# Storing dw1 through GpSimd's queue in pieces of 7, 117 and 4 rows

## The chip, the core and the metric

The kernel runs on one core of one Trainium2 chip. The core has five engines with a queue of instructions each: TensorE (PE in the profile, its weight loads PEld), VectorE (DVE), ScalarE (ACT), GpSimd (POOL) and SyncE (SP). Data move between the device memory and the on-chip memory (128 partitions) by 16 DMA engines, which all queues share; a transfer issued from SP and one issued from GpSimd stand in different DMA queues (q1 and q0 in the profile) of the same 16 engines. The metric is the device time of one execution in microseconds (us).

## The reference

The kernel computes one decoding step of a gated mix of two branches and all its gradients, for one token x of 640 numbers and the upstream gradient `grad_out`:

```python
g = _sigmoid((x * gate_w).sum(-1, keepdims=True))
a = _A_ref(x, A_k_cache, A_v_cache, A_wq, A_wo)   # attention, 32 heads x 4096 cached keys x 128
b = _B_ref(x, B_w1, B_b1, B_w2)                   # 640 -> 1728 -> 640, act = h * tanh(softplus(h))
return g * a + (1 - g) * b
...
_out, _vjp = jax.vjp(_f, A_x, A_k_cache, A_v_cache, A_wq, A_wo, B_w1, B_b1, B_w2, gate_w)
_grads = _vjp(grad_out)
```

Outputs are the result, and the gradients of x, both caches, wq, wo, w1, b1, w2 and the gate. Everything is bf16. The caches are 32 MB each, and so are their gradients dK and dV, so that the kernel reads 82 MB and writes 82 MB. The gradient of w1, dw1, is a matrix of 640 x 1728 in bf16, 2.2 MB: the outer product of x and the gradient dh of the hidden layer. The gradients of x and of the gate are rows of 640 numbers, like the result.

## The kernel before, in words

**Tiles.** A head's cache is one tile of 128 partitions x 8192 bytes, 1 MB in all; partition p holds 32 consecutive keys. dK and dV leave in tiles of the same shape. Weights are held with 128 of the 640 rows (or a group of rows) over the partitions: `w1_sb` is [128, 5, 1728], so that partition r holds the five rows r, 128 + r, ..., 512 + r of w1, each a run of 3456 bytes, and on the device these five runs lie 128 rows apart. The gradient dw1 is written into the same tile (`m_dw1`, line 499, on VectorE, one instruction for each of the five rows), and stored through the view `dw1_v` of the same shape.

**Loops.** The main loop (line 743) goes over the heads h = 0 to 30, the last head follows it by hand (lines 855 to 896). In each pass TensorE transposes the next head's tiles, multiplies for scores and for their gradient; ScalarE evicts and computes the exponentials; VectorE builds dV (`dv_out`) and dK (`dk_out`), two instructions of line 598 each, into a buffer of the pool `outs` (four buffers, tile name `o_sb`); from head 28 or 29 on the loads' own buffers (`Kn`, `Vn`) are used, since no more loads come. Heads go in groups of four; once a group, its parts of dwq and dwo are made and stored. The second branch's work stands in a list `mq`, from which `mlp_some` takes a few pieces in each pass; the five `m_dw1` are the last of it.

**Order and queues.** The order of instructions on each engine is that of the Python code; a framework adds the semaphore waits. All large transfers, loads and stores, are issued by SP in program order, and each waits for its data, for its buffer, and for the transfer eight places ahead of it. GpSimd issues a few small ones: the load of b1 in two parts, five small moves for the hidden layer, the last 64 rows of dw2 (line 800), db1 (line 802), and at the end three rows of results. DMAs issued from GpSimd use eight semaphores in turn as well.

**Around the change.** The last `m_dw1` runs in pass 26. In pass 30 (`h == H - 2`), after `dv_out(h, 1)` has issued its store on SP, SP issues dw1 in two transfers, of three and of two of the five rows of each partition (lines 805 and 806). At the very end, VectorE gathers the results of 15 x 128 numbers (`fin`), TensorE transposes them, ScalarE evicts them to `fin_rows`, a tile of 15 partitions, and GpSimd stores five partitions each to the result, to the gradient of x and to that of the gate (lines 920 to 922).

Of the kernel before, what the change touches and what calls it, by code (L numbers as in the profile page):

```python
# [16 lines left out]
def kernel(  # L17
# [24 lines left out]
    nc = tc.nc  # L42
    P = 128
    _, H, Sk, Dh = A_k_cache.shape
    D = A_x.shape[-1]
    F = B_w1.shape[1]
    assert Dh == P and Sk == 32 * P and D % P == 0 and H % 4 == 0 and H >= 16
    J = Sk // P
    RC = D // P
# [25 lines left out]
    dw1_v = out_6.rearrange("(rc r) f -> r rc f", r=P)  # L75
# [9 lines left out]
    out0_rows = out_0.rearrange("a b (c p) -> (a b c) p", p=P)  # L85
    out1_rows = out_1.rearrange("a b (c p) -> (a b c) p", p=P)
# [60 lines left out]
    w1_sb = const.tile([P, RC, F], BF16, name="w1_sb")  # L147
# [59 lines left out]
    def g_q(g):  # L207
        gp = groups[g]
        ps = grp([P, GD], F32, "q_ps")
        for rc in range(RC):  # L210
            nc.tensor.matmul(ps[:], lhsT=x_col_bf[:, rc:rc + 1].to_broadcast([P, P]),
                             rhs=wqs[g][:, rc, :], start=(rc == 0), stop=(rc == RC - 1))
        nc.scalar.copy(gp["q_row"][:], ps[:])
# [32 lines left out]
    def g_qpair_cp(g):  # L246
        pair_cp(qz, groups[g].pop("pair"), 4)

    def g_docol(g):
        groups[g]["col"] = col_mm(groups[g]["do_row"])  # L250

    def g_dopair(g):
        groups[g]["pair"] = pair_mm(groups[g].pop("col"))

    def g_dopair_cp(g):
        pair_cp(doz, groups[g].pop("pair"), 5)
# [25 lines left out]
    def f_new(g):  # L282
        gp = groups[g]
        gp["o_bf"] = grp_sb.tile([P, G], BF16, name="o_bf", tag="o_bf")
        gp["dq_bc"] = grp_sb.tile([P, GD], BF16, name="dq_bc", tag="dq_bc", bufs=1)

    def f_diag(g, a=0, b=G):
        gp = groups[g]
        if b == G:
            gp["o_sel"] = grp_sb.tile([P, G, P // 4], F32, name="o_sel", tag="o_sel", bufs=1)  # L290
            nc.vector.tensor_tensor(gp["o_sel"][:], seg[:].unsqueeze(1).to_broadcast([P, G, P // 4]),
                                    gp["dqo"][:, 1, :].unsqueeze(2).to_broadcast([P, G, P // 4]), ALU.mult)
        gp["dq_diag"] = g_diag(gp["dqo"][:, 0, :], scale, a, b)
# [76 lines left out]
    def f_dwq(g, c, a=0, b=G):  # L370
        cs = slice(a * Dh, b * Dh)
        nc.vector.tensor_scalar(wqs[g][:, c, cs], groups[g]["dq_bc"][:, cs], x_col_f[:, c:c + 1], None, ALU.mult)  # L372

    def f_dwq_st(g):
        for k, (a, z) in enumerate(WQP):
            if g == z - 1:
                nc.sync.dma_start(dwq_v[:, :, a * GD:z * GD], wqp[k][:])
# [140 lines left out]
    def ev():  # L518
        trq.pop(0)()
# [6 lines left out]
    def k_pe(h, c):  # L526
        if h < H:
            tr_pe(h, kts, KT, c)

    def v_pe(h, c):  # L530
        if h < H:
            tr_pe(h, vts, VT, c)
# [8 lines left out]
    def k_rows(h):  # L541
        rows_mm(KT.pop(h), qz[:, h % G], True)
# [22 lines left out]
    def softmax(h):  # L565
        mx = s_ps.tile([P, P + 2], F32, name="mx", tag="mx")
        nc.tensor.transpose(mx[:, 0:P], dgms.pop(h)[:].to_broadcast([P, P]), ident_f[:])  # L567
        negM = small.tile([P, 1], F32, name="negM", tag="negM")
        nc.vector.tensor_reduce(negM[:], mx[:, 0:P], axis=AX.X, op=ALU.max, negate=True)  # L569
        return mx, negM  # L570

    def exps(h, negM):
        es[h] = small.tile([P, J], BF16, name="e_bf", tag="e_bf")
        zds[h] = small.tile([P, 2], F32, name="zd", tag="zd")
        nc.scalar.activation(es[h][:], sd[h][0], ACT.Exp, bias=negM[:], scale=scale, accum_out=zds[h][:, 0:1])  # L575

    def pjs(h):
        pj = small.tile([P, J], F32, name="pj", tag="pj", bufs=2)
        nc.vector.scalar_tensor_tensor(pj[:], in0=sd[h][1], scalar=1.0, in1=es[h][:],  # L579
                                       op0=ALU.mult, op1=ALU.mult, accum_out=zds[h][:, 1:2])  # L580

    def zd_mm(h, mx):
        nc.tensor.matmul(mx[:, P:P + 2], lhsT=ones_f[:], rhs=zds[h][:], start=True, stop=True)  # L583
# [37 lines left out]
    def dk_out(h, k):  # L621
        if h >= 0:
            out_half("k", h, dKv, ds4s[h], groups[h // G]["qs_row"], k)
# [12 lines left out]
    def dqo_red(h, x):  # L636
        if h >= 0:
            v = x[:].rearrange("p t r -> p (t r)")[:, 3:3 + 4 * (P - 1)].rearrange("p (s q) -> p s q", q=P - 1)
            nc.vector.tensor_reduce(groups[h // G]["dqo"][:, :, h % G],  # L639
                                    v[:, :, 0:P - 1:32].rearrange("p s (i c) -> p i s c", i=2),  # L640
                                    axis=AX.XY, op=ALU.add)
# [101 lines left out]
    for h in range(H - 1):  # L743
        g, hh = h // G, h % G
        nx, pv = g + 1 < NG, g > 0
        k_pe(h + 1, 2)
        ev()
        mx, negM = softmax(h)
        if hh == 3 and nx:
            g_qpair_cp(g + 1)  # L750
            g_docol(g + 1)
        dqo_red(h - 1, xs[h])
        k_pe(h + 1, 3)
        ev()
        exps(h, negM)
        dk_out(h - 1, 1)
        v_pe(h + 1, 0)
        if hh == 2 and nx:
            g_q(g + 1)
        v_pe(h + 1, 1)  # L760
        if hh == 3 and nx:
            g_dopair(g + 1)
            g_dopair_cp(g + 1)
        k_rows(h + 1)
        ev()
        ev()
        pjs(h)
        v_pe(h + 1, 2)
        ev()
        zd_mm(h, mx)  # L770
        if hh == 0 and pv:
            f_new(g - 1)
            f_diag(g - 1)
        elif h >= 2:
            mlp_some(0.9, False)
        v_pe(h + 1, 3)
        ev()
        probs(h, mx)
        if hh == 0 and pv:
            f_o4(g - 1)  # L780
            f_o4c(g - 1)
            f_bc(g - 1)
        dv_out(h, 0)
        k_pe(h + 2, 0)
        dq_o(h)
        v_rows(h + 1)
        rw_cp(h + 1)
        if h + 2 < H:
            ev()
        dv_out(h, 1)  # L790
        load_k(h + KBUFS)
        load_v(h + VBUFS)
        k_pe(h + 2, 1)
        if h + 2 < H:
            ev()
        if h == H - 4:
            assert dw2_next[0] == FCN
            for a, b in W2P:
                nc.sync.dma_start(dw2_v[:, a:b, :], w2_sb[:, a:b, :])
            nc.gpsimd.dma_start(out_8[FM:F, :], w2_sb[0:FT, FR, :])  # L800
            assert not any(k == "bc" for k, _ in mq)
            nc.gpsimd.dma_start(db1_row, dh_bc[0:1, :])
        if h == H - 2:
            assert not mq
            nc.sync.dma_start(dw1_v[:, 0:3, :], w1_sb[:, 0:3, :])
            nc.sync.dma_start(dw1_v[:, 3:RC, :], w1_sb[:, 3:RC, :])
        dk_out(h, 0)
        x_tr(h + 1)
        maxes(h + 1)
        if hh == 0:  # L810
            if nx:
                g_new(g + 1)
            if pv:
                l_pe(g - 1, 0, G)
                l_add(g - 1, g - 1, True)
                for t in range(G):
                    f_dwo(g - 1, t)
                f_dwo_st(g - 1)
                for c in range(2):
                    f_dx(g - 1, c)  # L820
                    f_dwq(g - 1, c)
        if hh == 1:
            if pv:
                for c in range(2, RC):
                    f_dx(g - 1, c)
                    f_dwq(g - 1, c)
                f_dwq_st(g - 1)
            if nx:
                w_pe("o", g + 1, 0)
                ev()  # L830
                w_pe("o", g + 1, 1)
                ev()
        if hh == 2:
            if g + 2 < NG:
                load_wo(g + 2)
            if not nx:
                for k in range(NWT):
                    w_pe("q", g, k)
                    ev()
            else:  # L840
                w_pe("o", g + 1, 2)
                ev()
                g_do(g + 1)
                g_qcol(g + 1)
                g_qpair(g + 1)
        if hh == 3:
            if g % 2 == 0 and g + 4 <= NG:
                load_wqp(g // 2 + 1)
            if nx:
                g_qs(g + 1)  # L850
        if h >= 2:
            mlp_some(0.9 if hh < 2 else 1.8)
            dw2_some(2)
# [63 lines left out]
    nc.tensor.transpose(fin_ps[:], fin_bf[:], ident_bf[:])  # L917
    fin_rows = const.tile([3 * RC, P], BF16, name="fin_rows")
    nc.scalar.copy(fin_rows[:], fin_ps[:])
    nc.gpsimd.dma_start(out0_rows, fin_rows[0:RC, :])  # L920
    nc.gpsimd.dma_start(out1_rows, fin_rows[RC:2 * RC, :])
    nc.gpsimd.dma_start(out9_rows, fin_rows[2 * RC:3 * RC, :])


# [28 lines left out]
```

## Time and profile before

| what | us |
|---|---|
| median of 3 runs (lowest, highest) | 404.74 (404.52, 404.89) |
| profiled execution, its own time | 404.96 |
| its span, first to last instruction | 403.2 |
| busy: PE, DVE, ACT, POOL | 305.9, 287.9, 232.4, 11.8 |
| DMA, mean over the span | 408 GB/s, 164.55 MB |
| last `m_dw1` on VectorE starts | 325.9 |
| dw1 issued by SP (two transfers) | 375.0, 375.5 |
| rows issued by GpSimd | 393.7, 394.2, 394.7 |

How to read it: times in the profile count from the span's start. A slice or column is one fortieth of the stretch shown. "L598 DVE o_sb" is line 598 of the kernel on VectorE, writing tile `o_sb`; "[4.39 <-DMA out_dram<-o_sb]" behind an instruction says that its engine stood idle 4.39 us before it, until that DMA landed. A transfer's issue (SPq, POOLq, DMA_DIRECT2D) and its landing are two things: the issue takes the queue well under 2 us, the landing can come many us later, since the transfer stands in the queue of the DMA engines. A transfer is dealt over DMA engines, and each of them adds to its semaphore when its part has landed; the landing is the last of the sixteen increments. The chain of waits is followed back from the last instruction; time after the last instruction of the chain, until the last semaphore is in, belongs to no engine.

### The profile page before, as it was taken

How to read it: one execution, taken by the hardware profiler on the slowest of the kernel's cores; microseconds unless marked ns; L12 is line 12 of the kernel's file. 1: busy time of each engine (PE TensorE's matmuls, PEld its weight loads, DVE VectorE, ACT ScalarE, POOL GpSimd, SP SyncE). 2: the span in 40 equal slices, each digit the busy share in tenths (PEclk: the TensorE clock that was granted, in tenths of full speed). 3: DMA queues.
4: the chain of work that ended last, by engine and by line, in shares of the span. 5: the costliest groups of instructions: out<-in, count | busy, mean ns of one | idle time of the engine just before them, and what ended most of it. 6: DMA issues, size and time to landing. Idle time of an engine off the chain costs nothing.

```text
span 403.2 us, 7688 instructions
## 1 busy us (share of the span) xinstructions
PE 305.9 (76%) x2930; PEld 207.0 (51%) x2945; DVE 287.9 (71%) x808; ACT 232.4 (58%) x468; POOL 11.8 (3%) x29
## 2 busy tenths in 40 slices
PE   2979989787897985876887779876886977677640
PEld 1556646464565663544555447544555645464420
DVE  2217738868678875769897956896997985679780
ACT  2466757754676563753668667765767655375220
POOL 3000001000000000000001200000000000000001
PEclk9999999988999998989998997988999899889555
DMA  7999999999999999999999999999999999999894
GB/s 274 428 416 423 417 424 415 417 423 424 422 422 426 423 414 424 424 418 428 422 423 428 424 418 424 427 418 423 422 419 424 425 417 425 426 422 377 360 389 153
DMA packets 28708, 164.55 MB, mean 408 GB/s; under 512 B 2991, under 2 KB 3056, under 8 KB 12288
## 3 DMA queue, kind: packets, MB, share of 16 engines
q1 hardware_dynamic: 28256, 163.97, 98.1%
q8 instruction: 23, 0.38, 0.4%
q0 software_dynamic: 384, 0.10, 0.1%
q14 instruction: 13, 0.11, 0.1%
q10 hardware_dynamic: 32, 0.01, 0.0%
HBM read 82.03 MB, written 82.03 MB: 407 GB/s over the span
## 4 chain that ended last, share of the span: by engine, by line
DMA 42%; PE 25%; DVE 22%; ACT 6%; issue 2%; POOL 0%; POOLq 0%; SPq 0%; DVEq 0%; ACTq 0%
DMA out_dram<-o_sb 40%; PE tr L515 9%; DVE o_sb L598 9%; PE rw L538 3%; PE rw L631 3%; DVE junk L362 3%; DMA wq_p<-in_A_wq_dram 2%; PE x L555 2%; DVE wq_p L372 2%; ACT rw_sb L549 2%; ACT do_row L266 2%; PE tr L324 2%; PE do_ps L263 1%; PE h_ps L405 1%; DVE mjunk L494 1%
## 5 line engine op out<-in xcount | busy, mean ns | idle before, releaser
L524 ACT COPY T<-tr 128x512 f32<-128x512 f32 x256 | 138.0, 595 | 53.0 <-PE tr L515 38.3
L598 DVE TENSOR_TENSOR o_sb<-qs_row,ds 128x2048 bf16<-128x2048 bf16 x58 | 70.8, 1220 | 37.6 <-DMA out_dram<-o_sb 37.5
L515 PE MATMUL tr<-ident_f,Kn 128*128 128x128 f32 x512 | 85.6, 295 | 5.8 <-DVE rw L508 5.8
L515 PE MATMUL tr<-ident_f,Vn 128*128 128x128 f32 x512 | 84.5, 299 | 6.6 <-ACT T L524 6.0
L515 PEld LDWEIGHTS tr<-ident_f,Vn 128*128 128x128 f32 x512 | 63.4, 154 | 27.3 <-PE tr L515 12.1
L515 PEld LDWEIGHTS tr<-ident_f,Kn 128*128 128x128 f32 x512 | 61.1, 149 | 23.2 <-PE rw L631 14.1
L598 DVE TENSOR_TENSOR o_sb<-do_row,p 128x2048 bf16<-128x2048 bf16 x58 | 68.2, 1218 | 0.0
L549 ACT COPY rw_sb<-rw 128x512 f32<-128x512 f32 x33 | 19.4, 587 | 51.2 <-PE rw L538 49.0
L631 PE MATMUL rw<-Kn,ds 128*4 128x512 bf16 x256 | 35.9, 405 | 6.4 <-DVE ds L593 5.7
L631 PE MATMUL rw<-Vn,p 128*4 128x512 bf16 x256 | 35.9, 405 | 0.0
L567 PE MATMUL mx<-ident_f,m_s 128*128 128x128 f32 x32 | 10.1, 316 | 29.7 <-DVE m_s L563 29.6
L555 PE MATMUL x<-ident_f,rw_sb 128*128 128x128 f32 x132 | 22.5, 295 | 4.4 <-ACT rw_sb L549 1.4
L362 DVE SCALAR_TENSOR_TENSOR junk<-wq_p,dq_bc 128x512 bf16<-128x512 bf16 x35 | 23.9, 684 | 0.0
L538 PE MATMUL rw<-T,qz 128*32 128x512 bf16 x256 | 22.3, 426 | 0.0
L575 ACT ACTIVATE e_bf<-x,negM 128x32 bf16<-128x32 f32 x32 | 9.3, 292 | 22.4 <-DVE dqo L639 22.1
L567 PEld LDWEIGHTS mx<-ident_f,m_s 128*128 128x128 f32 x32 | 4.5, 142 | 34.0 <-DVE m_s L563 33.9
L538 PE MATMUL rw<-T,doz 128*32 128x512 bf16 x256 | 21.4, 411 | 0.8 <-ACT T L524 0.8
L380 ACT ACTIVATE wo_g<-da_bc,o 128x640 bf16<-128x640 bf16 x28 | 20.9, 816 | 1.2 <-PE ax_ps L350 1.2
L583 PE MATMUL mx<-zd,ones_f 128*128 128x2 f32 x64 | 11.2, 245 | 13.5 <-DVE pj L579 13.4
L555 PEld LDWEIGHTS x<-ident_f,rw_sb 128*128 128x128 f32 x132 | 14.5, 145 | 13.2 <-ACT rw_sb L549 13.2
L569 DVE TENSOR_REDUCE negM<-mx 128x1 f32<-128x128 f32 x32 | 9.2, 288 | 16.1 <-PE mx L567 16.1
L631 PEld LDWEIGHTS <-ds 128*4 128x4 bf16 x256 | 9.1, 85 | 22.2 <-DVE ds L593 11.4
(174 smaller groups left out, 367.6 us busy)
## 6 DMA issues: line engine op xcount, KB each, us to landing
out_dram<-o_sb SPq DMA_DIRECT2D x58, 1024.0 KB, 16.6
Kn<-in_A_k_cache_dram SPq DMA_DIRECT2D x32, 1024.0 KB, 16.8
Vn<-in_A_v_cache_dram SPq DMA_DIRECT2D x32, 1024.0 KB, 17.3
wq_p<-in_A_wq_dram SPq DMA_DIRECT2D x4, 1280.0 KB, 8.7
wo_g<-in_A_wo_dram SPq DMA_DIRECT2D x8, 640.0 KB, 17.6
out_dram<-wo_g SPq DMA_DIRECT2D x8, 640.0 KB, 18.3
out_dram<-wq_p SPq DMA_DIRECT2D x4, 1280.0 KB, 16.3
out_dram<-Kn SPq DMA_DIRECT2D x3, 1024.0 KB, 11.4
```

What stands on the lines that cost most here:

```text
L362: nc.vector.scalar_tensor_tensor(jq[:], in0=wqs[g][:, c, :], scalar=1.0, in1=groups[g]["dq_bc"][:], op0=ALU.mult, op1=ALU.mult, accum_out= ...
L380: nc.scalar.activation(wos[g][:, hh, :], da_bc[:], ACT.Copy, scale=groups[g]["o4"][:, hh:hh + 1])
L515: nc.tensor.transpose(tp[:, t, :], words[:, t * P:(t + 1) * P], ident_f[:])
L524: nc.scalar.copy(T[h][:, (3 - c) * (TB // 2):(4 - c) * (TB // 2), :], tp[:])
L538: nc.tensor.matmul(rw[32 * c:32 * (c + 1), :], lhsT=z[:, par, :, :].rearrange("p m u -> p (m u)"), rhs=Tb[:, c, par, :, :], start=first an ...
L549: nc.scalar.copy(rw_sb[h][:].rearrange("p t r -> p (t r)"), rw[:])
L555: nc.tensor.transpose(xs[h][:, 3 - j, :], t[:, j, :], ident_f[:])
L567: nc.tensor.transpose(mx[:, 0:P], dgms.pop(h)[:].to_broadcast([P, P]), ident_f[:])
L575: nc.scalar.activation(es[h][:], sd[h][0], ACT.Exp, bias=negM[:], scale=scale, accum_out=zds[h][:, 0:1])
L583: nc.tensor.matmul(mx[:, P:P + 2], lhsT=ones_f[:], rhs=zds[h][:], start=True, stop=True)
L598: nc.vector.tensor_tensor(dst[:, a:b, :].rearrange("p j (k t) -> p j k t", t=4), row.rearrange("p (k t) -> p k t", t=4).unsqueeze(1).to_br ...
L631: nc.tensor.matmul(rw[32 * c:32 * c + 4, :], lhsT=c4[:, 4 * jb:4 * jb + 16].rearrange("p (j t) -> p t j", t=4)[:, 0, :], rhs=N[:, jb:jb + ...
```

## The change

The two SP transfers of dw1 go. In their place, at the same spot of the program but in GpSimd's queue, three transfers store partitions 0 to 6, 7 to 123 and 124 to 127 of `w1_sb`, each with all five rows (runs of 3456 bytes) of its partitions. At the end the result's five rows and the first three of the gradient of x are each stored as two runs of 64 numbers (128 bytes) a row instead of one run of 128 numbers, the last two rows of the gradient of x by a transfer of their own, and the gradient of the gate as before. No computation changes. The built programs differ on no engine but GpSimd and SP: GpSimd issues four more transfers, SP two fewer.

```diff
+    def st_cut(dst, src, cuts, run):
+        for a, b in zip(cuts, cuts[1:]):
+            nc.gpsimd.dma_start(dst[a:b], src[a:b], max_dma_last_dim=run)
...
         if h == H - 2:
             assert not mq
-            nc.sync.dma_start(dw1_v[:, 0:3, :], w1_sb[:, 0:3, :])
-            nc.sync.dma_start(dw1_v[:, 3:RC, :], w1_sb[:, 3:RC, :])
+            st_cut(dw1_v, w1_sb[:], (0, 7, 124, P), 2 * F)
         dk_out(h, 0)
...
     nc.scalar.copy(fin_rows[:], fin_ps[:])
-    nc.gpsimd.dma_start(out0_rows, fin_rows[0:RC, :])
-    nc.gpsimd.dma_start(out1_rows, fin_rows[RC:2 * RC, :])
+    st_cut(out0_rows, fin_rows[0:RC, :], (0, RC), P)
+    st_cut(out1_rows, fin_rows[RC:2 * RC, :], (0, 3), P)
+    nc.gpsimd.dma_start(out1_rows[3:RC, :], fin_rows[RC + 3:2 * RC, :])
     nc.gpsimd.dma_start(out9_rows, fin_rows[2 * RC:3 * RC, :])
```

`run` is the greatest length of a run in bytes: 3456, one row of w1, for dw1, and 128 for the output rows.

## The prediction

> **What bounds the kernel now.** First the page's slices: one column is 10.1 us.
>
> ```profile
> span 403.2 us, 7688 instructions
> ...
> DMA  7999999999999999999999999999999999999894
> GB/s 274 428 416 423 417 424 415 417 423 424 422 422 426 423 414 424 424 418 428 422 423 428 424 418 424 427 418 423 422 419 424 425 417 425 426 422 377 360 389 153
> ```
>
> The DMA engines are full from the second column to the last but four, at some 422 GB/s: what decides is when transfers land. From column 37 on they are not always full; there the chain of waits tells what ends last:
>
> ```profile
> 325.88 18.48 DMA out_dram<-o_sb
> 344.46 1.23 DVE o_sb L598
> ...
> 393.67 0.53 POOL out_dram L920
> 394.20 0.51 POOL out_dram L921
> 394.71 0.49 POOLq L948
> ```
>
> To 344.46 the chain goes from store to store: VectorE waits for a store to free an o_sb buffer. After that it is computation to the end, with no DMA in it; so whatever delays 344.46 delays 393.67. But the chain stops 8 us before the span's end. What fills those is in the DMA view of the window 396 to 404 (a column is 0.2 us) and in the landing of the last dwo store:
>
> ```profile
> GB/s 384 399 256 83 46 46 46 31 20 22 31 20 32 20 22 31 20 31 20 31 20 26 51 26 26 26 26 26 0 0 0 0 0 0 0 0 0 0 0 0
> ```
>
> ```profile
> L386 SPq DMA_DIRECT2D out_dram<-wo_g x1: 393/393/393, 390.7 to 390.7; - x1
> ...
> DMA to landing us min/median/max: 11.4/11.4/11.4
> ```
>
> 422 GB/s over 16 engines is 26 each: from 397.4 to 401.6 one engine works alone. The trace's landing records hold sixteen increments per transfer: of this store fourteen came by 397.11, one at 397.83, the last at 402.16. The same engine is behind earlier: of the store on the chain (issued 325.88) fourteen increments came by 339.06, one at 339.94 and the last at 344.37. So one late engine, some 5 us behind, sets both the wait that ends at 344.46 and the end of the span. What its share of a transfer is, and when, is what this change is worth.
>
> **The change, part by part.** The profiled execution took 404.96 us, span and 1.76 around it; the median of the runs shown is 404.74. I work in the span and add the difference to the median.
>
> ```profile
> 325.88 0.67 DVE L499 TENSOR_SCALAR w_sb<-dh_bc,cols_f 128x1728 bf16<-128x1728 bf16 x1
> ...
> 344.46 1.23 DVE L598 TENSOR_TENSOR o_sb<-qs_row,ds 128x2048 bf16<-128x2048 bf16 x1 [4.39 <-DMA out_dram<-o_sb]
> ```
>
> ```profile
> 375.03 0.43 SPq L805 DMA_DIRECT2D out_dram<-w_sb  x1
> 375.51 0.99 SPq L806 DMA_DIRECT2D out_dram<-w_sb  x1
> 380.59 0.34 SPq L616 DMA_DIRECT2D out_dram<-Kn  x1
> ```
>
> *Removed from SP:* two issues, 0.43 and 0.99. SP's next store goes out at 380.59, when VectorE ends its input, so nothing in SP's queue gains by it: 0.
>
> *Moved to GpSimd's queue:* the wait there is for the fifth L499, which ends at 326.55, 48 us before SP's issue. Nothing stands behind it on GpSimd before the output rows at 393.67, so the wait holds up nobody. An issue costs it 0.5 to 0.6 (these rows):
>
> ```profile
> 291.88 0.57 POOL L800 DMA_DIRECT2D out_dram<-w_sb  x1 [68.10 <-ACT w_sb L503]
> ...
> 393.67 0.53 POOL L920 DMA_DIRECT2D out_dram<-fin_rows  x1 [100.69 <-ACT fin_rows L919]
> ```
>
> Three make 1.7 us of idle time: 0. L800's increments came 4.6 to 5.5 us after issue, so the pieces move from about 331 on, beside SP's full queue. Writing the runs' addresses (640 runs against L800's 64) may start them later; that only eases what follows.
>
> *The bytes themselves:* 2.2 MB now run at 331 to 351 and no longer at 375 to 390. One of the 128 rows (five runs of 3456 B) costs the late engine 0.71 us: of the two dw1 stores before, eight rows of it, the last increments came at 387.63 and 389.95, after 384.28 of the store ahead, so 5.67 / 8. Elsewhere it is (384.00 - 378.62) / 8 = 0.67. Call s the rows that the late engine gets; an even deal is 8. Then the landing at 344.37 moves by 0.71 s (its packets alternate with the other queue's) and its last landing by 0.71 (s - 8).
>
> The cuts are 7, 117 and 4. Every transfer of the trace is dealt in equal shares, and 117 has none over 16 engines, but has over 13 of nine rows; 7 and 4 give one row each to seven and four. Then three engines get nothing of the large piece. If the deal goes on where the last piece ended, starting at the first engine, these three are the fifth to seventh; s is 2 there and 9 or 10 elsewhere. The late engine holds a row in each of the three five-row stores at the end (its 256-byte packets stand at 397.99, 398.49 and 398.99), so it is one of the first five. Whether it is the fifth no row tells. I take s = 2, between 0 and 10 as ends. My reason is the equal shares; a hint is that in the first five-row load four engines begin at 1.708 to 1.716 and the fifth at 1.741.
>
> - At 344.46: plus 2 x 0.71 = 1.4. Bounds: 0, if the pieces come after it, and 2.2, if the engines with ten rows become the late ones (339.94 + 10 x 0.67 = 346.6 against 344.37). Every step of the chain moves with it, since it has no DMA wait after that.
> - Late engine's end: 402.16 - 6 x 0.71 = 397.9. The next engine's: 397.83 + 2 x 0.67 = 399.2 at most.
>
> *The output rows:* four issues instead of three on the chain's end, so the last goes out at 394.70 + 0.5 + 1.4 = 396.6. Half-length runs (128 B) are 13 or 15 more packets of under 20 ns: 0. From issue to landing it was 2.98 on the other engines (394.70 to 397.68) and 4.84 on the late one (399.54). With that backlog gone I take 2.98: 399.6; the bound is 401.4. This is now the last landing.
>
> *Sum:* 399.6 + 1.02 (402.16 to the end 403.18) = 400.6, 2.6 less than before: 404.74 - 2.6 = 402.1. With the bounds (0 and 2.98; 2.2 and 4.84) the case reaches from 400.7 to 404.8.
>
> The Trainium skill, "DMA: Bandwidth & Descriptors", section "Why a DMA increments its semaphore by 16 and not by 1", lets a copy use the largest number of engines up to 16 that divides its outer sizes, and on GpSimd's path consecutive ones from a cursor that moves on; by it s is 2 for the fifth engine, and the sum is as above. The same paragraph has an exception: some direct copies of GpSimd go over all sixteen with the rows per engine rounded up; by it s is 1 + 8 + 1 = 10. The five-row stores agree with the exception (a moving cursor would have given the late engine one row of the three); no row here shows the first rule.
>
> **Rivals.**
>
> *Slower: the late engine gets 9 or 10 rows.* For it: if each piece starts at the first engine, as the three five-row stores do, any of the first five gets 1 + 8 or 9 + 1; so too in a deal that goes on, if it is the first to fourth. Against: 117 would have to be dealt unevenly, or four of five places hit. At 331 the late engine has 13.4 us of queue ahead of the landing at 344.37; one packet of 0.14 after each of 0.31 stretches this to 19.4, so VectorE goes on at 350.4, 6.0 later. The last output row goes out at 394.70 + 0.5 + 6.0 = 401.2, lands at 404.2 to 406.0, and the span is 405.2 to 407.1: 406.7 to 408.6, middle 407.7. By end = 399.2 + 0.71 s it is slower from six rows on.
>
> The skill's same page, section "Latency and other measured facts", names the eighth and sixteenth engine (7 and 15) as the usually slower; the eighth would get 9 + 1 rows and the time would be this rival's. The trace disagrees so far as the late engine is among the first five dealt.
>
> *No change.* The three pieces begin late, or the engines with ten rows give back what the late one gains: the wait at 344.46 grows by some 4 us, or s is 5 or 6. Against: 9 or 10 rows instead of 8 are only 1.3 us, and these engines have 4.4 to 5 to spare. 404 to 405.5.
>
> *The move does nothing at the end, as the output rows set it.* The last row lands at 399.54 before, 2.6 ahead of the dwo store, so there is 2.6 to gain and no more; it is why the sum is not 4.3.
>
> **How the numbers follow.** Two rows for the late engine: 0.62 (0.58 below 403.9, 0.03 within, 0.01 above); nine or ten rows: 0.33; no change: 0.05 (0.03 within, 0.02 slower). The split of the first two is more choice than calculation, since the late engine's place is not in the trace. Two parts in a thousand, 0.8 us, is about what a measurement of this kernel can tell from no change: faster 0.58, same 0.06, slower 0.36. The range runs from just under the first case's end, 400.6, to the middle of the slower one, 407.7: half of 0.33 and a little at the foot are left out. The likeliest case alone: 400.7 to 404.8.
>
> **What would show it.** Right: dw1's issues on GpSimd at about 326.6 to 328; VectorE's wait ends by 346; in the last 8 us no stretch of one engine alone; the dwo store lands within 9 us of its issue, and an output row is the last to land. Wrong: VectorE's wait for o_sb lasts to 350 (the late engine got its full share early), or the lone engine still works after 400.

## The result and the profile after

The changed kernel is slower: median 407.62 us (404.33 to 409.79, 18 runs) against 404.76 (404.48 to 405.69, 18 runs), ratio 1.0067, 95% interval 1.0049 to 1.0084. The forecast was 402.1. The profiled execution took 407.63, with a span of 405.8 (before 404.96 and 403.2).

From the page of the changed kernel (from about line 377 on, its line numbers are three or four higher than before):

```profile
span 405.8 us, 7705 instructions
...
DMA  7999999999999999999999999999999999999857
GB/s 276 429 415 425 415 414 422 414 423 424 421 423 424 423 414 424 418 422 425 425 421 428 424 420 423 422 421 424 428 422 423 426 408 355 383 425 424 341 237 286
```

The columns are full as before, but columns 33 to 35 (325 to 355 us) read 408, 355 and 383 where before had 417, 425 and 426. The engines were busy there and moved less. The last columns are lower too, 341 to 237: now the DMA waits for computation. The chain of waits:

```profile
325.54 25.33 DMA out_dram<-o_sb
350.97 1.23 DVE o_sb L602
...
395.98 1.19 DVE wo_g L387 x4
400.13 1.16 POOL out_dram L376 x2
```

VectorE and GpSimd in order of time:

```profile
350.97 1.23 DVE L602 TENSOR_TENSOR o_sb<-qs_row,ds 128x2048 bf16<-128x2048 bf16 x1 [11.24 <-DMA out_dram<-o_sb]
```

```profile
326.50 2.25 POOL L376 DMA_DIRECT2D out_dram<-w_sb  x3 [33.90 <-DVE rz L591]
400.13 1.16 POOL L376 DMA_DIRECT2D out_dram<-fin_rows  x2 [71.39 <-ACT fin_rows L922]
401.29 0.55 POOL L925 DMA_DIRECT2D out_dram<-fin_rows  x1
401.83 0.54 POOL L926 DMA_DIRECT2D out_dram<-fin_rows  x1
```

The same store, issued at 325.54 (before 325.88), lands 6.5 us later, and the stall ahead of L602 is 11.24 us instead of 4.39. From there to the first output row it is 400.13 - 350.97 = 49.2 us, as before (393.67 - 344.46 = 49.2). So the chain's delay of 6.5 us arises entirely in this one wait. The span grows by 2.6 only, since the end gains. The end of this execution looks as forecast. The DMA view of 396 to 406 (a column is 0.25 us) falls from full to nothing:

```profile
GB/s 524 492 393 262 426 492 295 295 328 385 385 410 377 385 393 385 401 393 385 385 393 479 385 389 451 389 410 369 32 6 0 0 0 0 0 0 0 0 0 0
```

No lone engine is left here. The landing records of the last dwo store hold sixteen increments from 403.39 to 403.63; before they were spread over 5.2 us. The last output row lands at 404.37 and is the last transfer to land.

What happened between 331 and 345 is in the table of windows (window, length, busy us and instructions of PE, PEld, DVE, ACT, POOL, then the granted TensorE clock, DMA share, GB/s). Before:

```profile
331.00:345.00 14.00, 8.80 (x90) 5.95 (x88) 7.31 (x21) 6.95 (x13) 0.00 (x0) 1.00 1.02 422
```

After:

```profile
331.00:345.00 14.00, 8.46 (x89) 5.86 (x87) 6.62 (x20) 6.95 (x13) 0.00 (x0) 1.00 1.02 365
```

The DMA share is the same, 365 GB/s instead of 422. In the packet records, the 8 KB packets of caches and gradients that start in this window take 369 ns in the mean instead of 310; the median is 309 in both, but 14% take over 500 ns, against one of 584 before. The pieces' own packets are of 6912 bytes, two runs of 3456; between 330 and 348 they take 305 ns in the mean, with a median of 262.

The packets also show how the pieces were dealt. GpSimd's queue has 308 packets of 6912 bytes and 24 of 3456. An engine with n rows has 5n runs: one row makes two pairs and a single, nine rows make 22 pairs and a single. 7 x 2 + 13 x 22 + 4 x 2 = 308, and 7 + 13 + 4 = 24: equal shares over 7, 13 and 4 engines. The engines without a share are not left out altogether. With the old row stores (the run "dw1 only" below) the queue also has, from 320 on, 108 packets of 8 bytes, 9 x 2 + 3 x 22 + 12 x 2: as many as the 9, 3 and 12 engines without a share would have had as pairs.

### The profile page after: what moved, and what is told of

It reads as the page before. It is cut to its first block, busy times and chain, and to the rows that moved or that the text cites. A ratio compares the mean times of both kernels' runs of the same rounds, so it can differ in the third digit from the quotient of the medians.

```text
span 405.8 us, 7705 instructions
## 1 busy us (share of the span) xinstructions
PE 306.2 (75%) x2945; PEld 206.1 (51%) x2945; DVE 287.9 (71%) x808; ACT 232.8 (57%) x468; POOL 14.7 (4%) x33
## 4 chain that ended last, share of the span: by engine, by line
DMA 48%; DVE 23%; PE 21%; ACT 4%; issue 2%; POOL 0%; POOLq 0%; SPq 0%; DVEq 0%; ACTq 0%
DMA out_dram<-o_sb 46%; DVE o_sb L602 9%; PE tr L519 7%; DVE junk L362 3%; PE rw L635 3%; PE rw L542 3%; DMA wq_p<-in_A_wq_dram 2%; DVE wq_p L372 2%; PE x L559 2%; PE tr L324 1%; ACT rw_sb L553 1%; ACT do_row L266 1%; PE do_ps L263 1%; PE h_ps L409 1%; DVE mjunk L498 1%
## 5 line engine op out<-in xcount | busy, mean ns | idle before, releaser
L602 DVE TENSOR_TENSOR o_sb<-qs_row,ds 128x2048 bf16<-128x2048 bf16 x58 | 70.8, 1220 | 45.2 <-DMA out_dram<-o_sb 45.2
L519 PE MATMUL tr<-ident_f,Kn 128*128 128x128 f32 x512 | 84.4, 292 | 5.7 <-DVE rw L512 5.7
L519 PEld LDWEIGHTS tr<-ident_f,Vn 128*128 128x128 f32 x512 | 63.8, 155 | 26.2 <-PE tr L519 12.7
L602 DVE TENSOR_TENSOR o_sb<-do_row,p 128x2048 bf16<-128x2048 bf16 x58 | 68.2, 1218 | 0.0
L587 PE MATMUL mx<-zd,ones_f 128*128 128x2 f32 x64 | 11.2, 245 | 13.6 <-DVE pj L583 13.5
```

Source lines behind the costliest of these rows:

```text
L519: nc.tensor.transpose(tp[:, t, :], words[:, t * P:(t + 1) * P], ident_f[:])
L602: nc.vector.tensor_tensor(dst[:, a:b, :].rearrange("p j (k t) -> p j k t", t=4), row.rearrange("p (k t) -> p k t", t=4).unsqueeze(1).to_br ...
```

## The experiments

Each edit is given against the changed kernel. "Old rows" means the kernel's old stores of the output rows:

```diff
-    st_cut(out0_rows, fin_rows[0:RC, :], (0, RC), P)
-    st_cut(out1_rows, fin_rows[RC:2 * RC, :], (0, 3), P)
-    nc.gpsimd.dma_start(out1_rows[3:RC, :], fin_rows[RC + 3:2 * RC, :])
+    nc.gpsimd.dma_start(out0_rows, fin_rows[0:RC, :])
+    nc.gpsimd.dma_start(out1_rows, fin_rows[RC:2 * RC, :])
```

Each ratio is against the kernel before on the same chip (its medians there were 404.7 to 405.0). "Wait ends" is the end of VectorE's stall behind the store that was issued at about 326.

| run | dw1: pieces, queue, issued at | wait ends | GB/s while dw1 runs | median us | ratio, 95% interval |
|---|---|---|---|---|---|
| one transfer, early | 128, GpSimd, 327 | 349.95 | 424 | 405.92 | 1.0022, 1.0013 to 1.0031 |
| rows only | as before, SP, 375 | 344.26 | 386 | 404.86 | 0.9997, 0.9989 to 1.0006 |
| cuts on SP | 7/117/4, SP, 375 | 344.16 | 329 | 406.76 | 1.0039, 1.0027 to 1.0051 |
| dw1 only, old rows | 7/117/4, GpSimd, 327 | 348.49 | 364 | 407.85 | 1.0072, 1.0058 to 1.0086 |
| cuts late | 7/117/4, GpSimd, 373 | 344.98 | 320 | 405.99 | 1.0031, 1.0020 to 1.0043 |
| one transfer, late | 128, GpSimd, 373 | 345.17 | 394 | 405.43 | 1.0016, 1.0007 to 1.0024 |
| changed kernel again | 7/117/4, GpSimd, 327 | 350.88 | 363 | 407.82 | 1.0074, 1.0056 to 1.0092 |
| cuts at 11 | 11/117, GpSimd, 328 | 353.27 | 349 | 409.52 | 1.0123, 1.0108 to 1.0138 |
| halves | 64/64, GpSimd, 327 | 350.82 | 347 | 406.82 | 1.0047, 1.0034 to 1.0060 |
| by rows of five | 128 x 2, 2, 1 rows, GpSimd, 314, 326, 328 | 350.10 | 421 | 405.57 | 1.0021, 1.0012 to 1.0030 |
| cuts at 352 | 7/117/4, GpSimd, 352 | 344.74 | 364 | 403.82 | 0.9979, 0.9968 to 0.9990 |
| one transfer at 352 | 128, GpSimd, 352 | 344.70 | 424 | 405.29 | 1.0014, 1.0005 to 1.0023 |

Waits and GB/s are those of the profiled execution, which is one of the runs behind the median. The GB/s are those of 331 to 345, 356 to 372 or 374 to 388, as the transfer lies; the kernel before has 422, 393 and 378 there, the last with its own dw1 stores on SP.

### Which part costs: the place, the cuts or the rows

**One transfer, early**, with the old rows:

```diff
-            st_cut(dw1_v, w1_sb[:], (0, 7, 124, P), 2 * F)
+            st_cut(dw1_v, w1_sb[:], (0, P), 2 * F)
```

> dw1 from GpSimd's queue at the same place, but as one transfer of 128 rows (eight rows for each DMA engine), output rows as in the kernel before. Theory A, the early start costs: 2.2 MB at 331 to 351 delay the landing for which VectorE waits, whatever the cut; eight rows cost the late engine 5.7 us, the wait ends near 350, the time is 406 to 408. Rival B, the uneven cuts cost: with an even deal the wait ends by 346.5 and the time is 404 to 405.5.

VectorE and the window of 331 to 345:

```profile
349.95 1.22 DVE L602 TENSOR_TENSOR o_sb<-qs_row,ds 128x2048 bf16<-128x2048 bf16 x1 [9.71 <-DMA out_dram<-o_sb]
```

```profile
331.00:345.00 14.00, 9.54 (x86) 6.30 (x85) 6.77 (x20) 6.28 (x13) 0.00 (x0) 0.89 1.02 424
```

Eight rows for every engine put the wait's end 5.5 us later, against 8 x 0.71 = 5.7 by the prediction's formula. So the formula holds where packets keep their length: 424 GB/s, and the 6912-byte packets take 263 ns. Yet the time rises by only 0.2%, to just under the 406 that was expected at least. The chain ends at 397.1 where it ended at 393.7, and at the end the late engine is 1.6 to 1.7 us behind instead of 4.3. The DMA was waiting for computation (a busy share of 0.73 from 374 to 388, before 0.93), and that gives the late engine time to catch up.

**Rows only**: dw1 on SP as before, the new stores of the rows.

```diff
-            st_cut(dw1_v, w1_sb[:], (0, 7, 124, P), 2 * F)
+            nc.sync.dma_start(dw1_v[:, 0:3, :], w1_sb[:, 0:3, :])
+            nc.sync.dma_start(dw1_v[:, 3:RC, :], w1_sb[:, 3:RC, :])
```

> The kernel before with the new stores of the output rows alone. Theory A: the fourth transfer (0.5 us) and the short runs hide behind the late engine's dwo store, which lands 2.6 us after the last row: 404.6 to 405.0, no change. Rival C, the output rows cost by themselves: 405.3 or more, and an output row lands last.

404.86 against 405.03 in the same batch, 0.9997: the rows cost nothing that can be measured. Here dwo was issued at 388.44, 2.3 us earlier than before, and its last increment came at 401.98 all the same. While the late engine sets the end, a chain of computation some 2 us shorter is worth nothing.

**Cuts on SP**, at dw1's old place, with the old rows:

```diff
-            st_cut(dw1_v, w1_sb[:], (0, 7, 124, P), 2 * F)
+            for a0, b0 in ((0, 7), (7, 124), (124, P)):
+                nc.sync.dma_start(dw1_v[a0:b0], w1_sb[a0:b0])
```

> The three pieces of 7, 117 and 4 rows on SP's queue at the old place (375), output rows as before. If the late engine is among those that get nine or ten rows, its last landing moves by 0.7 to 1.4 us: 405.4 to 406.2. If it is among the three passed over by the large piece, its last landing moves by -4 us or more and the rows' landing (399.5) ends the span: 402 to 402.7. An even deal of 117 leaves 404.7 to 405.

Slower by 0.4%, with the wait untouched. The DMA view of 396 to 406:

```profile
GB/s 377 321 268 264 293 241 220 144 164 153 119 127 98 123 94 102 115 94 107 70 70 98 82 82 61 61 61 41 0 0 0 0 0 0 0 0 0 0 0 0
```

The time is above all three bands that were expected, the nearest being 405.4 to 406.2. The engines end one after another up to 403.5, 1.3 after the 402.16 of before. Two rows of 0.67 would make that, ten instead of eight for the late engine, as pieces that each start at the first engine give to the fifth, sixth or seventh (1 + 9); which engine was the last here is not shown. And the window of 374 to 388 moves 329 GB/s at the same busy share of 0.93 as before (378): the cuts slow the DMA on SP's queue as well, so it is not GpSimd's queue that does it.

**Dw1 only**: the changed kernel with the old rows.

> The three pieces from GpSimd's queue, output rows as before (three transfers). Theory A: 0.5 us less than the changed kernel, about 407. If the deal of pieces goes on from one execution to the next (24 engines in all here, 24 + 8 in the changed kernel), single times scatter between about 402 (late engine passed over) and 409 (it gets ten rows), more widely than the changed kernel's; if each transfer starts at the first engine, they agree within 1 us.

407.85, ratio 1.0072: the whole loss is dw1's. The half us that the old rows were expected to save is not there. Its six runs lie between 405.44 and 408.93; the profiled one is the fastest, with a wait to 348.49. The kernels with early cuts scatter more than the one before (404.33 to 409.79 against 404.48 to 405.69). The 3.5 us here lie between the two expectations, 402 to 409 if the deal wanders and within 1 us if it does not.

### When the pieces go

**Cuts late**: a small copy on GpSimd, which must wait for a tile of pass 30, holds the pieces back.

```diff
+            nc.gpsimd.tensor_copy(hold[:], p4s[h][:, 0, :])
             st_cut(dw1_v, w1_sb[:], (0, 7, 124, P), 2 * F)
```

> The changed kernel, but GpSimd first copies a few numbers that VectorE makes in pass 30, so that the three pieces start near 373 as SP's stores did, and not at 331. Theory A (the early start costs): VectorE's wait for o_sb ends at 344 to 345 again; the end is set by the late engine alone, 405.4 to 406.2 where it gets nine or ten rows, 402 to 402.7 where the large piece passes it over. Rival B (the uneven deal or the queue costs wherever it stands): 407 to 408.5 as for the changed kernel.

**One transfer, late**: the same with `(0, P)` and the old rows.

> The same hold, but one transfer of 128 rows (eight for each engine), output rows as before. Theory A: the same bytes at the same time as in the kernel before, from another queue: 404.5 to 405.4. Rival B (GpSimd's queue costs by itself, since its packets of two runs displace SP's): 405.9 as with the early start of the whole, or more.

Both have the wait back at 345. The single transfer keeps the late engine: dwo's last increment comes at 402.83, 5.1 after the others. Its 405.43 lies between the two bands that were expected. With cuts no engine is alone, but dwo's increments are spread from 397.41 to 402.99 and the window of 374 to 388 falls to 320 GB/s. So the cuts relieve the late engine and slow the others by as much, right where no time is left to recover it. Neither is faster than before. The 405.99 of the cuts is in an expected band, but in that of a late engine with nine or ten rows.

**The changed kernel again**, on the same chip:

> The changed kernel again, for a second profile and for how its times scatter on one chip. If the place where the deal of the pieces starts differs from execution to execution (theory D), single times scatter over 3 us or more (kernel before: 1 us), and which engine is passed over differs between this profile and the first. If it is always the same (rival E), single times agree within 1.2 us as with the even deal.

407.82, with the same wait (to 350.88) and rate (363 GB/s). The times lie within 2.5 us, between what was expected if the start of the deal varies (3 or more) and if it is fixed (1.2). The end differs from that of the first profile. The DMA view of 396 to 406:

```profile
GB/s 393 221 385 410 360 401 393 385 393 377 393 385 385 377 369 504 352 463 414 373 373 332 51 23 20 41 20 20 20 1 0 0 0 0 0 0 0 0 0 0
```

Here one engine does work alone, from 401.6 to 403.2: fifteen increments of dwo come from 401.81 to 402.00, the last at 403.58, and the last output row lands with that engine at 404.31. The chain from 350.88 to the first output row (398.58) took 47.7 us and not 49.2, and the span is 405.8 all the same. That the first profile has no lone engine is thus not the cuts' doing alone.

### Whether the late engine is passed over

**Cuts at 11**: two pieces, of 11 and 117 partitions.

```diff
-            st_cut(dw1_v, w1_sb[:], (0, 7, 124, P), 2 * F)
+            st_cut(dw1_v, w1_sb[:], (0, 11, P), 2 * F)
```

> Pieces of 11 and 117 rows instead of 7, 117 and 4: again 24 engines' worth, but the large piece begins four engines further on, so that other three are passed over. Theory D (the start varies): median and scatter as for the changed kernel, 406.5 to 408.5, within 0.7 us of its median on the same chip. Rival E (fixed start): another time than the changed kernel's, by 1 us or more, with a scatter below 1.2 us.

The wait ends later still, and the late engine is the last everywhere (shown by its lag, below). The median is 1.7 us above the changed kernel's, as a fixed start asked for; the times lie within 1.7 us, not 1.2. The profiled execution is the slowest of the four (410.88), and its store went out at 326.99, 1.1 us later than before; from issue to landing it took 26.2 us against 18.5, 7.7 more.

```profile
353.27 1.22 DVE L602 TENSOR_TENSOR o_sb<-qs_row,ds 128x2048 bf16<-128x2048 bf16 x1 [12.10 <-DMA out_dram<-o_sb]
```

The late engine can be told in the landing records by its lag, which grows from transfer to transfer while the distances between the others stay: before from 9.40 to 9.83 us behind the first engine, over transfers whose first part lands at 347 to 369. In the changed kernel one increment grows so, from 4.16 to 4.95 over 357 to 377, while the last one stays at 9.25 to 9.31; the repeat shows the same (from 3.95 to 4.77, and 9.28 to 9.31). With the cut at 11 the last one itself grows, from 10.8 to 11.2 over 366 to 378. By this mark pieces of 7 pass over the late engine and pieces of 11 do not. A deal that goes on, from the first engine, leaves the fifth to seventh out of the large piece after 7 and the ninth to eleventh after 11; both fit a late engine among the fifth to seventh, and so does the 10 of the cuts on SP. Its identity is read from this pattern only; no record names the engine.

### Why the DMA slows

**Halves**, equal shares of four rows for every engine, twice, with the old rows:

```diff
-            st_cut(dw1_v, w1_sb[:], (0, 7, 124, P), 2 * F)
+            st_cut(dw1_v, w1_sb[:], (0, P // 2, P), 2 * F)
```

> GpSimd stores dw1 at the early place in two pieces of 64 partitions, with the old stores of the output rows. Each piece gives each of the 16 engines four rows, so each engine has eight rows of dw1 as with the one transfer of 128 partitions (405.9). Theory A (packets of two engines get into each other's way where a piece's rows are not dealt over the 128 partitions as those of SP's stores are): 64 partitions are dealt otherwise than 128, so from 331 to 345 the DMA moves well under 422 GB/s (360 to 400) and 8 KB packets take over 330 ns in the mean; VectorE's wait for o_sb ends at 351 or later, and the time is 406.5 to 408.5. Theory B (the slow stretch of the changed kernel comes from unequal shares or from the engines' counts 7, 13 and 4): shares are equal here, 420 GB/s or more, packets of 310 ns, wait to 350, 405.5 to 406.5.

**By rows of five**, three pieces over all 128 partitions, with the old rows:

```diff
-            st_cut(dw1_v, w1_sb[:], (0, 7, 124, P), 2 * F)
+            nc.gpsimd.dma_start(dw1_v[:, 0:2, :], w1_sb[:, 0:2, :])
+            nc.gpsimd.dma_start(dw1_v[:, 2:4, :], w1_sb[:, 2:4, :])
+            nc.gpsimd.dma_start(dw1_v[:, 4:RC, :], w1_sb[:, 4:RC, :])
```

> Three pieces from GpSimd at the early place, each over all 128 partitions (two, two and one of the five rows of each partition), old stores of the output rows. As many issues as in the changed kernel, all dealt like SP's stores. If three issues, or three transfers in GpSimd's queue, cost something by themselves, 406.5 or more and a throughput from 331 to 345 under 415 GB/s; if the slow stretch comes from how the pieces' partitions are dealt, as one whole transfer: 422 to 425 GB/s, VectorE's wait to 349.5 to 350.5, 405.5 to 406.3.

The window of 331 to 345, first the halves, then by rows of five:

```profile
331.00:345.00 14.00, 8.71 (x89) 5.86 (x87) 6.71 (x20) 6.95 (x13) 0.00 (x0) 1.00 1.02 347
```

```profile
331.00:345.00 14.00, 8.89 (x63) 6.63 (x62) 4.41 (x18) 5.39 (x12) 0.00 (x0) 0.76 1.02 421
```

In the halves the 6912-byte packets take 364 ns in the mean, by rows of five 265 (one transfer 263, the changed kernel 305). The test by rows is weaker than it was meant to be: its first two rows of five were ready early and issued at 313.87, so that only 162 of its 320 packets fall into the window. While that first piece ran (315 to 323) the rate was 424 GB/s, so three issues show no cost; but for the same bytes from the same queue at the same time the comparison is that of the halves with one transfer. Both give every engine eight rows of 3456-byte runs: 347 against 424 GB/s, and the fifteenth increment of the store that VectorE waits for comes at 347.52 instead of 344.89. So unequal shares are not needed; pieces that do not cover all 128 partitions are enough. Both times lie in the bands that were expected for them; the 347 GB/s of the halves are lower than the 360 to 400 expected. The Trainium skill offers a mechanism: in "SBUF — State Buffer", section "Door 1: The DMA port swizzle (why `[64,N]` ≈ `[32,N]`)", partitions 0 to 63 reach only half of the memory's 16 DMA ports, and in "DMA: Bandwidth & Descriptors", section "The descriptor swizzle", a transfer of 128 partitions gives each engine a port of its own. Where a piece is dealt otherwise, two engines could then meet at one port. The packets of about twice 309 ns agree with that; no run here shows the ports themselves, and the halves also change which rows of device memory are written together, which was not taken apart.

### Is there a place where the cuts pay

**Cuts at 352**: held back like the late cuts, but to pass 28, whose branch (`h == H - 4`) now holds the pieces. They go out at 352, after the store for which VectorE waits has landed.

```diff
             nc.gpsimd.dma_start(db1_row, dh_bc[0:1, :])
-        if h == H - 2:
             assert not mq
+            nc.gpsimd.tensor_copy(hold[:], p4s[h][:, 0, :])
             st_cut(dw1_v, w1_sb[:], (0, 7, 124, P), 2 * F)
```

> The changed kernel with the pieces of 7, 117 and 4 partitions held back, by a small copy on GpSimd that reads the p tiles of pass 28, to about 352 us: after the store that VectorE waits for (its wait should end at 344.5 to 345.5 as before), and 20 us before the later place at which they gave 406.0. Theory: the pieces cost in three ways, as work ahead of that store, as packets that slow each other while they run, and, issued at 373, as packets still slow at the end. At 352 the first and third are gone and the late engine is still relieved: the throughput falls to 350 to 380 GB/s from 356 to 372, the dwo store's sixteen increments lie within 1.5 us, and the time is 402.5 to 404.2, below both kernels. Rival: the bytes that the slow packets displace reach the end all the same, dwo lands at 402 to 403.5 and the time is 404.5 to 406.

**One transfer at 352**, the same with `(0, P)` and the old rows:

> As the kernel with the pieces held to 352 us, but dw1 goes as one transfer of 128 partitions, dealt eight rows to each engine, with the old stores of the output rows. Theory (the late engine is relieved by the cuts even at 352, and the cuts' slow packets cost less than that there): without the cuts the late engine has all its work, the dwo store's last increment comes 4.8 to 5.4 us after the others as before, the throughput from 356 to 372 is 420 GB/s or more, and the time is 404.5 to 405.4, above the 403.8 of the cuts. Rival (the gain at 352 is that of the time of issue, through GpSimd's queue and past SP's eight places, and the cuts have no part in it): 403.5 to 404.3, and the late engine no more than 4.2 us behind at the end.

VectorE with the cuts at 352, and the window of 356 to 372:

```profile
344.74 1.23 DVE L602 TENSOR_TENSOR o_sb<-qs_row,ds 128x2048 bf16<-128x2048 bf16 x1 [4.38 <-DMA out_dram<-o_sb]
```

```profile
356.00:372.00 16.00, 12.08 (x101) 8.20 (x99) 12.75 (x37) 10.31 (x23) 0.00 (x0) 0.89 1.00 364
```

And the DMA view of 396 to 406, first with the cuts at 352, then with one transfer at 352:

```profile
GB/s 377 418 373 297 149 123 128 67 86 46 45 45 26 29 41 20 20 20 42 0 0 0 0 0 0 0 0 0 0 0 0 0 0 0 0 0 0 0 0 0
```

```profile
GB/s 33 34 33 0 26 26 25 25 25 25 25 25 33 25 25 25 25 41 20 20 20 41 20 0 0 0 0 0 0 0 0 0 0 0 0 0 0 0 0 0
```

With one transfer the late engine works alone from before 396 to 401.6: dwo's last increment comes at 402.19, 6.2 after the next. With the cuts the others work to 399.35 and the late one to 401.37, 2.0 after the next. The time falls to 403.82 against 404.68 before, ratio 0.9979 (0.9968 to 0.9990), better than both kernels; one transfer at the same place gives 405.29 against 404.81. The two differ in the row stores as well, which cost nothing that can be measured (rows only). So the relief of the late engine is worth something, about 0.9 us against the kernel before, once the pieces stay out of the way of the store that VectorE waits for. The slow packets take part of it: 364 GB/s instead of 424. Both theories' marks were missed in part: dwo's increments lie 4.1 us apart, not 1.5, but the time is below the rival's 404.5. The profiled execution took 404.44, more than the median of the twelve (402.42 to 405.20).

## Why the prediction was wrong, step by step

**The bound** (one late engine sets the wait's end and the span's end): right. With one transfer at 352 or at 373 its last increment still comes 5 to 6 us after the others, and a chain 2 us shorter bought nothing while it was there (rows only).

**Removed from SP, moved to GpSimd's queue, 0 each:** the issues came at 326.50, 327.15 and 328.12, as forecast, and nobody waited behind them. One transfer in GpSimd's queue at 352 or 373 costs 0.14% to 0.16%, however; that is some 0.6 us which the sum had at nothing, and for which the runs give no cause (with a small copy on GpSimd ahead of it, and at another time than SP's).

**The deal:** right. 308 and 24 packets are equal shares over 7, 13 and 4 engines. This is the first rule of the Trainium skill's "DMA: Bandwidth & Descriptors", section "Why a DMA increments its semaphore by 16 and not by 1", and not its exception; it held for these pieces here. The five-row stores started at the same engine each time, and no run shows what decides between the two. The prediction's 10 rows under the exception hold for the first four engines only; the fifth, which has no row of the last piece, would get 1 + 8 = 9. That the late engine was passed over (s = 2) is borne out by the growing lag, by the cut at 11, and by the 4.2 us less that it is behind with the cuts at 352 than with one transfer there (2.0 against 6.2, and six rows of 0.71 are 4.3).

**At 344.46, plus 1.4 and at most 2.2: this is the step that failed.** It came out at 6.5. The upper bound priced the engines with nine or ten rows at 0.67 a row on top of their old landing, 339.94 + 6.7 = 346.6. That price was read from stores over all 128 partitions, and so the bound trusted that packets keep their length beside pieces that are dealt otherwise. It was 347.29 for the second last engine, and 350.88 for the last, which by its constant lag is not the late one. Half of the store's sixteen increments had come by 337.0 before and by 344.4 after, 7.4 later where the nine or ten rows make 6.0 to 6.7. What is over the rows we put down to the slow packets: 365 GB/s instead of 422 over 14 us is 0.8 MB, or 1.9 us of all engines together. At equal rows they cost 2.6 us at the second last engine (the halves against one transfer). How many of them the last engine had, no record tells. A second queue alone is not the reason: with one transfer from GpSimd's queue the same formula was right to 0.2 us.

**The end:** right in kind. In the first profile no late engine sets it, the row issues cost 0.54 to 0.58 each, and the last row took 404.37 - 401.83 = 2.54 to land (2.98 forecast). With 6.5 in the place of 1.4 the sum of the prediction gives 400.6 + 5.1 = 405.7; the span is 405.8. So one term carries the miss, though two smaller ones cancel beside it (the landing 0.44 shorter, and 1.48 instead of 1.02 from it to the end). The halved runs of the rows made no more packets: there are 15 of 256 bytes, as before. But the balance at the end proves less than it seems: with one transfer early, with no cut and the chain 3.4 us later, the late engine is down to 1.7 us too. A later end of the chain relieves it by itself. And in the repeat of the changed kernel, whose chain ended 1.6 earlier, one engine was again alone to 403.2; by its lag, which stayed the same up to 377, it was not the late one, and why it was so far behind is open.

**The rivals.** The slower one had the time (407.7) and the wait's end (350.4), but by another road: the late engine with nine or ten rows. That road exists, with the cut at 11, and gives 409.5 and 353.27. Its packets of 0.14 between SP's were one run each; GpSimd's queue sent two runs in one of 0.26, so that ten rows are done in 25 rounds, 6.6 us instead of 6.0. "No change" named part of what happened, the engines with ten rows giving back what the late one gains; it set 4 us of wait to cancel the gain and had a chance of 0.05, since those engines had 4.4 to 5 us to spare. They used 6 to 7 for the rows and more for the slow packets. What a grown wait costs is less than its growth: one transfer early, with 5.5 us of it, ends 0.9 later, and the changed kernel, with 6.5 us and no late engine, 2.9 later.

**The chances:** 0.36 for slower was too little. The sign hung on a bound in which one price, that of packets beside pieces on differently dealt partitions, had been taken from transfers over all 128.

## What to carry to other kernels

Where the DMA is full, moving a store ahead of another one delays that one by the moved rows on every engine; look first at who waits for the transfer that is overtaken, and let the moved store follow it. An uneven deal can relieve a late DMA engine, but pieces that do not cover all 128 partitions slowed everything that ran beside them here (320 to 365 GB/s instead of 378 to 424), so place them where there is time to recover, some 50 us before the end and not 30. A price taken from transfers over all 128 partitions is no bound for pieces dealt otherwise, whether they come from the same queue (329 GB/s) or from another (347 to 365); a whole transfer from the other queue kept the price here (424).

## What the runs showed of the hardware that was not expected

- Pieces of 7, 117 and 4, of 11 and 117, and of 64 and 64 partitions lowered the DMA's rate at an unchanged busy share of 1.01 to 1.02: from 422 to 365, 349 and 347 GB/s. Pieces over 128 partitions left it at 421 to 424. With the pieces of 7, 117 and 4, up to 14% of the neighbouring 8 KB packets took over 500 ns instead of 309.
- GpSimd's queue sent two runs of 3456 bytes as one packet of 6912 bytes, in 262 ns at the median, so that a row of five runs is two packets and a half; an engine without a share of a piece got as many packets of 8 bytes (108 for the pieces of 7, 117 and 4).
- The late engine catches up at the end as soon as the DMA has to wait for computation: from 9.5 us behind the first engine at 360 to 5.2 at the end before, and to 1.8 with one transfer early and the chain ending 3.4 us later.
